# The output projection of a gated mix of FNet and sliding-window attention, by Strassen's scheme on pairs of blocks instead of block by block

## The chip, the cores and the metric

The kernel runs on one core of one Trainium2 chip. The metric is device time in microseconds of that core, median of three runs. Engines are named as in the profile: PE is TensorE, PEld its weight loads, DVE VectorE, ACT ScalarE, POOL GpSimd, SP SyncE (which issues DMAs). L528 is line 528 of the kernel before; of the changed kernel, lines are a little higher where the same code moved (L528 is L529 there, L453 is L454, L587 is L588).

## The reference

With S = 2048 positions of D = 512, 32 heads of 16 and a causal window of 256:

```python
a = x @ dft_hid_re.T;  b = x @ dft_hid_im.T
y = dft_seq_re @ a - dft_seq_im @ b            # FNet
q, k, v = heads(x @ wqkv)
p = softmax(where(0 <= i - j < 256, q k^T / 4, -1e9))
attn = (p @ v) @ wo                            # sliding-window attention
g = sigmoid(sum(x * gate_w))
out = g * y + (1 - g) * attn
```

## The kernel before, in words

All data are fp32, kept as two parts: `hi`, the value cast to the matmul's fp32r type, and `lo`, the rest (`lo = x - hi`). A product takes three matmuls, `hi hi`, `hi lo`, `lo hi`: TERMS. A "split" is a cast (L80 on ACT, L82 on DVE) and a subtraction on DVE (L85).

PE's order is written out by hand (a manual schedule of PE alone; the other engines' orders come from the scheduler, and each engine runs its own in turn). It weaves two streams. The **dense** stream has the projections of x, then `y`: for each block of 128 positions 16 chunks of three matmuls of 512 columns (`c_part`, L528, result `dc`). The pieces of the DFT matrices `cr` and `ci` (512 KB each) are loaded to `raw`, a pair of buffers, and split there to `hi` and `lo` by jobs between matmuls (L115 and L116, in the profile at L587 `late`). The **attention** stream walks over 128 blocks `n` (4 groups of 8 heads by 16 blocks of the sequence, two heads at a time): `s_pair` (L366) for block n, and for block k = n - LAG, `t_pair` (L448), whose probabilities `pt` or `home` are written by ACT (L449) and masked by POOL's affine selects (L453, L457). Every six blocks a visit of `pv` (L474) multiplies them with `vpad`, into which POOL spreads v (L431). `make_pad` (L349, DVE) writes the pads that `s_pair` and `t_pair` read. The attention's output goes to DRAM (`o_scr`), and the sum of gate times `y` to `r_scr` or, where the projection is ahead, to `mixed`.

The loop of attention ends with `attention_done`: `wo` (512 by 512, as two halves of 512 KB) is loaded through `raw`, split on DVE into `fin`, which takes the place of `ring0`, a buffer of attention's own; `os` takes that of `ring1`. From then on `FIN` is set, and `c_part` calls `tail_step()` ahead of every four chunks, that is every 12 dense matmuls. A tail step runs `wo_block` for up to two blocks: 12 matmuls of 128x512 each (4 head groups by TERMS, L811) into a bank of PSUM of `ps_a`, then on DVE `r = (1 - g) * ps + r` (L813), and the block's 256 KB go out by SP. Then it prepares more blocks (`wo_prep`: the block of `o_scr` is loaded, ACT casts it, DVE subtracts). Blocks 15 and 14 go first of those still missing their `y`, so that their attention part stands ready. The last block of `y` ends in two column halves of 256 (`c_final`, L558, 12 matmuls), whose two results are added at L560 and leave on SP's and ACT's queues (L561).

Of the kernel before, what the change touches and what calls it, by code (L numbers as in the profile page):

```python
# [7 lines left out]
F32 = mybir.dt.float32  # L8
F32R = mybir.dt.float32r
AF = mybir.ActivationFunctionType  # L10
OP = mybir.AluOpType
# [21 lines left out]
def fnet_window_mix(ctx: ExitStack, tc: tile.TileContext, xT, x, wqk, wv, wr, wi, cr, ci, wo, gw, out):  # L33
# [509 lines left out]
    def c_final(get, ab):  # L543
        ps = ps_d.tile([P, 512], F32, name="dc", tag="d")
        g = g1[:, 15:16]
        for j in range(2):
            w = get((1, 30 + j))
            yield from c_part(w, range(16)[8 * j:8 * j + 8 - 2 * j], ab, ps, (0, 13))
            yield
        while wait:  # L550
            tail_step()
        r = mixed.pop(15)
        late(nc.vector.scalar_tensor_tensor, r, ps, g, r, OP.mult, OP.add)
        for c, dma in ((slice(0, 256), nc.sync), (slice(256, 512), nc.scalar)):
            ps2 = ps_a.tile([P, 512], F32, name="t", tag="st")
            for i in (14, 15):
                for a, b in TERMS:
                    nc.tensor.matmul(ps2[:, c], w[a][:, i % 8 * 128:i % 8 * 128 + 128], ab[SC[i]][:, b, c],  # L558
                                     start=i == 14 and a + b == 0, stop=i == 15 and a == 1)
            nc.vector.scalar_tensor_tensor(r[:, c], ps2[:, c], g, r[:, c], op0=OP.mult, op1=OP.add)  # L560
            dma.dma_start(out[15][:, c], r[:, c])  # L561
        yield
# [22 lines left out]
    def late(fn, *args):  # L585
        with behind("act", "dve"):
            return fn(*args)  # L587
# [172 lines left out]
    now = []  # L760
    wait = []
    mixed = {}
    born = {}
    clock = iter(range(99))

    def tail_step():
        t = next(clock)
        for tb in [tb for tb in O if born[tb] < t - 2][:2]:
            if tb in wait:
                wait.remove(tb)  # L770
                ld(out[tb], wo_block(tb, 1))
            else:
                mixed[tb] = wo_block(tb, 0)
        for tb in (*wait[:5], 15, 14, *wait[5:]):
            if tb not in O and tb not in mixed and len(O) < 7 and (tb > now[-1] or tb in wait):
                wo_prep(tb)
                born[tb] = t

    def attention_done():
        fin = const.tile([P, 8192], F32R, name="fin", tag="ring0")  # L780
        ORAW.extend(f(fin[:, 4112 + 512 * i:4624 + 512 * i]).rearrange("p (g t) -> p g t", g=NG) for i in range(7))
        fin = fin[:, 16:4112].rearrange("p (j c h e) -> p j c h e", j=2, c=2, h=2)
        OS.append(const.tile([P, 8, 2, NG, P], F32R, name="os", tag="ring1"))
        for j in range(2):
            raw = st.tile([P, 1024], F32, name="raw", bufs=2)
            ld(raw, wo[j])
            for c in range(2):
                split(fin[:, j, c, 0], fin[:, j, c, 1], raw[:, c * 512:c * 512 + 512])
        FIN.append(fin)

    OS = []
    ORAW = []
    O = {}
    slot = iter(range(99))

    def wo_prep(tb):
        oraw = ORAW[0]
        ORAW.append(ORAW.pop(0))
        ld(oraw, o_scr[tb // 4][:, :, tb % 4 * P:tb % 4 * P + P].rearrange("g p t -> p g t"))
        O[tb] = OS[0][:, next(slot) % 8]  # L800
        split(O[tb][:, 0], O[tb][:, 1], oraw[:], True)

    def wo_block(tb, half):
        o = O.pop(tb)
        r = ev.tile([P, 512], F32, name="ev")
        ld(r, r_scr[half if half or tb < 16 - SWITCH else 2][tb])
        ps = ps_a.tile([P, 512], F32, name="t", tag="st")
        n = 0
        for g in range(NG):
            for a, b in TERMS:  # L810
                nc.tensor.matmul(ps, o[:, a, g], FIN[0][:, g // 2, g % 2, b], start=n == 0, stop=n == 11)  # L811
                n += 1
        nc.vector.scalar_tensor_tensor(r, ps, g0[:, tb:tb + 1], r, op0=OP.mult, op1=OP.add)  # L813
        return r


    stream = dense()
# [39 lines left out]
    def v_next(n):  # L857
        if n < N:
            for c in range(2):
                need(("v", n % NB // 2 + c))  # L860
            with behind(*(("sp",) if n < 8 else ())):
                v_load(n)

    for n in range(N + LAG + 1):
        k = n - LAG
        if k == 0:
# [8 lines left out]
        for p in range(NP):  # L875
# [11 lines left out]
            if visit:  # L887
                for j in range(summed, k):
                    pv(j)
                summed = k  # L890
                if k < N:
                    t_pair(k, p)
            for at_n, at_p, do in TURN if n > 12 else FIRST:
# [61 lines left out]
```

## Time and profile before

| | us |
|---|---|
| median of 3 runs (lowest to highest) | 851.23 (850.59 to 851.45) |
| the profiled execution, own time | 850.96 |
| its span in the trace | 849.0 |
| PE busy | 843.7 (99%) |
| DVE, ACT, POOL busy | 611.3, 593.6, 256.8 |
| output projection, first and last matmul of L811 | 774.0 to 837.2, x192 |

The page's first part gives each engine's busy time. PE's matmuls overlap in the pipeline, so the duration of one (392 ns for 512 columns) is not the time that it takes from the stream; that is the distance between two starts. The granted clock is that of TensorE, 1.00 at full speed. A row of the chain of waits says from when on, and for how long, an instruction group was what the end waited for. A row of the timeline has start, length, engine, line, operation, tiles, shapes and count.

### The profile page before, as it was taken

What the parts mean: (1) busy time and instruction counts of PE and PEld (TensorE: products, weight loads), DVE (VectorE), ACT (ScalarE), POOL (GpSimd) and SP (SyncE); (2) the same over time, 40 slices, a digit from 0 to 9 for tenths busy, and PEclk for the clock granted to TensorE, in tenths of its full rate; (3) what the DMA queues carried; (4) which work ended last, traced back from release to release, by engine and by line L of the source; (5) the groups of instructions that cost most, each with busy time, mean ns of one, the idle gap of its engine ahead of it and who ended that gap; (6) DMA issues with size and microseconds to landing.
All of it is one profiled execution on the core that took longest, in us unless ns stands there. A gap on an engine that the chain in (4) does not pass through costs nothing.

```text
span 849.0 us, 16711 instructions
## 1 busy us (share of the span) xinstructions
PE 843.7 (99%) x5166; PEld 691.4 (81%) x5166; DVE 611.3 (72%) x1999; ACT 593.6 (70%) x1798; POOL 256.8 (30%) x578
## 2 busy tenths in 40 slices
PE   9999999999999999999999999999999999999998
PEld 6888888888888788888888887888887878878887
DVE  5588978667978787787787886887987864437531
ACT  6488888878888897787877886877777865532100
POOL 8102332233332233342323333343233364620000
PEclk9999999999999999999999999999999999999999
DMA  8776678476765275533454557969774435339732
GB/s 296 244 228 186 214 243 257 181 233 225 216 222 178 63 211 134 171 115 123 137 158 127 177 150 227 308 216 306 254 215 134 138 121 164 128 118 333 225 134 75
DMA packets 94345, 160.99 MB, mean 190 GB/s; under 512 B 26800, under 2 KB 35760, under 8 KB 94256
## 3 DMA queue, kind: packets, MB, share of 16 engines
q1 hardware_dynamic: 93824, 159.28, 60.2%
q8 instruction: 40, 0.66, 0.3%
q10 hardware_dynamic: 432, 0.66, 0.2%
q14 instruction: 49, 0.40, 0.1%
HBM read 108.27 MB, written 51.64 MB: 188 GB/s over the span
## 4 chain that ended last, share of the span: by engine, by line
PE 94%; DMA 2%; DVE 2%; issue 1%; SPq 0%; ACT 0%; DVEq 0%; ACTq 0%
PE dc L528 39%; PE dqk L280 9%; PE dab L303 9%; PE t L448 9%; PE s L366 8%; PE o L474 8%; PE t L811 5%; PE dv L303 5%; DMA raw<-wo 1%; DMA ev<-l_scr 1%; PE s L268 1%; DVE sm L368 1%; PE dv L592 0%; SPq L56 0%; DVE pad L349 0%
## 5 line engine op out<-in xcount | busy, mean ns | idle before, releaser
L528 PE MATMUL dc<-big,hi 128*128 128x512 f32 x1020 | 344.5, 393 | 0.0
L371 ACT ACTIVATE sm<-sm,ml 128x320 f32<-128x320 f32 (+4 forms) x512 | 277.4, 543 | 59.6 <-DVE ml L368 54.1
L368 DVE CUSTOM_DVE_ANT_0 sm<-s,mask 128x320 f32<-128x320 f32 (+4 forms) x512 | 235.0, 464 | 108.6 <-PE s L366 73.2
L449 ACT ACTIVATE pt<-t 128x320 f32<-128x320 f32 (+4 forms) x392 | 159.8, 411 | 87.7 <-PE t L448 82.1
L528 PE MATMUL dc<-big,lo 128*128 128x512 f32 x510 | 200.3, 393 | 0.0
L528 PEld LDWEIGHTS dc<-big,hi 128*128 128x128 f32 x1020 | 180.4, 188 | 22.6
L448 PE MATMUL t<-ring,pad 128*128 128x320 f32 (+4 forms) x512 | 156.8, 306 | 0.1
L453 POOL TENSOR_SCALAR_AFFINE_SELECT pt<-pt 128x128 f32<-128x128 f32 x196 | 71.2, 363 | 283.3 <-ACT pt L449 279.7
L366 PE MATMUL s<-ring,pad 128*128 128x320 f32 (+4 forms) x512 | 155.3, 303 | 0.3 <-DVE ml L368 0.2
L349 DVE TENSOR_SCALAR pad<-ring,half 96x256 fp32r<-96x256 f32 x384 | 120.4, 360 | 11.9 <-PE t L448 11.7
L448 PEld LDWEIGHTS t<-ring,pad 128*128 128x128 f32 x512 | 96.1, 188 | 31.1 <-issue 8.7
L366 PEld LDWEIGHTS s<-ring,pad 128*128 128x128 f32 x512 | 96.2, 188 | 21.7 <-DVE ml L368 2.0
L528 PEld LDWEIGHTS dc<-big,lo 128*128 128x128 f32 x510 | 95.9, 188 | 11.9
L371 ACT ACTIVATION_READ_ACCUMULATOR sm<-sm,ml 128x1 f32 x512 | 97.4, 190 | 0.0
L587 DVE TENSOR_TENSOR lo<-raw,hi 128x512 fp32r<-128x512 f32 x137 | 93.8, 694 | 0.1
L303 PE MATMUL dab<-hi,big 128*128 128x512 f32 x256 | 89.0, 394 | 0.0
L280 PE MATMUL dqk<-big,hi 128*128 128x512 f32 x240 | 85.0, 393 | 0.0
L431 POOL TENSOR_SCALAR vpad<-vr,half 128x256 f32<-128x256 f32 x64 | 61.3, 969 | 65.3 <-PE o L474 30.3
L587 DVE CAST hi<-raw 128x512 fp32r<-128x512 f32 x137 | 57.7, 431 | 20.5 <-PE dc L528 17.0
L347 ACT ACTIVATE pad<-ring,half 96x256 fp32r<-96x256 f32 x128 | 66.8, 522 | 0.0
L457 POOL TENSOR_SCALAR_AFFINE_SELECT pt<-pt 128x128 f32<-128x128 f32 x172 | 60.8, 354 | 0.0
L474 PE MATMUL o<-pt,vpad 128*32 128x320 f32 (+4 forms) x1072 | 57.7, 351 | 0.0
(96 smaller groups left out, 912.5 us busy)
## 6 DMA issues: line engine op xcount, KB each, us to landing
qk_scr<-home SPq DMA_DIRECT2D x32, 512.0 KB
ring<-qk_scr SPq DMA_DIRECT2D x32, 512.0 KB
raw<-cr SPq DMA_DIRECT2D x32, 512.0 KB
raw<-ci SPq DMA_DIRECT2D x32, 512.0 KB
r_scr<-ev SPq DMA_DIRECT2D x42, 256.0 KB
ev<-r_scr SPq DMA_DIRECT2D x42, 256.0 KB
ab_scr<-home SPq DMA_DIRECT2D x20, 512.0 KB
big<-ab_scr SPq DMA_DIRECT2D x20, 512.0 KB
```

Of the source, the lines that this page charges most:

```text
L280: nc.tensor.matmul(ps, w[a][:, c:c + 128], XT[dk, ss][:, b], start=n == 0, stop=n == 11)
L303: nc.tensor.matmul(ps, XT[dk, ss][:, a, c * 128:(c + 1) * 128], wh[b], start=n == 0, stop=n == 11)
L349: nc.vector.tensor_scalar(dst, src, half[:96, h:h + 1], None, op0=OP.mult)
L366: nc.tensor.matmul(ps[:, :w], PAD[0, n][:, p], ring[1][:, p, k0:k0 + w], start=True, stop=True)
L368: mark("dve", nc.vector.tensor_tensor_reduce(out=sm[:, :w], in0=ps[:, :w], in1=mask[:, WIN - w:], scale=1.0, scalar=3e38, op0=OP.add, op1= ...
L371: mark("act", nc.scalar.activation(sm[:, :w], sm[:, :w], AF.Exp, bias=nm[:, c], scale=-1.0, accum_out=l[:, c]))
L448: nc.tensor.matmul(ps[:, :w], PAD[1, n][:, p], ring[0][:, p, q0:q0 + w], start=True, stop=True)
L449: nc.scalar.activation(pt[:, p, :w], ps[:, :w], AF.Exp, scale=-1.0)
L453: nc.gpsimd.affine_select(a, a, pattern=[[0, 2], [2, 64]], compare_op=OP.is_ge, fill=0.0, base=1, channel_multiplier=-1)
L474: nc.tensor.matmul(OT[g, sb][32 * p:32 * p + 32, q - sb * 512:e - sb * 512], v2[:, p], pt[:, p, q - q0:e - q0], start=first, stop=kb == 8 ...
L528: nc.tensor.matmul(ps, w[a][:, i % 8 * 128:i % 8 * 128 + 128], ab[SC[i]][:, b], start=i == ends[0] and a + b == 0, stop=i == ends[1] and a ...
L587: return fn(*args)
```

## The change

The output projection is done for pairs of blocks (0 and 1 the first two finished, 15 and 14 the third pair, eight in all). The attention output of a pair, 256 by 512, times `wo`, 512 by 512, is seen as a 2x2 by 2x2 product of halves (128 positions by 256 by 256) and done in Winograd's form of Strassen's scheme: 7 products instead of 8. A product is 2 (chunks of 128 in the inner dimension) times 3 (TERMS) matmuls of 128x256, so a pair takes 42 of them instead of 24 of 128x512. Four sums of the operand's halves, s1 to s4, are made on POOL (`sums`) and the seven operands split (ACT's casts, DVE's subtractions) into columns of ring0 and ring1; the seven weight operands are made once: four differences for each of the two chunks of the inner dimension on POOL (`wo_diffs`, L827), and in all 14 casts and 14 subtractions on DVE (`fin_split`). The products are combined on the way to the result: ACT copies p1 to `u` (L934), DVE adds p6 to it (L936), and `into` (L928) adds with the gate to `r`, seven times a pair.

A pair is begun in one tail step (`wo_begin`, 24 matmuls, products p1, p6, p7, p5 in four banks) and ended in the next one (`rest`, 18 matmuls that go on in three of these banks); the steps are listed in `BEGIN`. The sums are issued three steps earlier, the splits one step, the loads of the attention output four.

What `attention_done` did is moved ahead: `wo` is fetched chunk by chunk (2 x 256 KB each) in blocks 114 and 117 of k (through `raw`, in turn with the pieces of `ci`), its differences and splits follow in blocks 115 to 120 into columns of the rings that attention has left, the first pair is loaded, summed and split in blocks 121 to 123 (`BEFORE_END`). From `FIN` on the casts of the dense stream's pieces are done by ACT instead of DVE. The result of a pair is kept in `rt` (in place of `home`), the operand in buffers that `vpad` and the pads leave.

```diff
-            jobs.append(lambda c=c: late((nc.vector if masks else nc.gpsimd).tensor_copy, hi[:, c], raw[:, c]))
+            jobs.append(lambda c=c: late(nc.scalar.copy if FIN else (nc.vector if masks else nc.gpsimd).tensor_copy,
+                                         hi[:, c], raw[:, c]))
...
     def tail_step():
         t = next(clock)
-        for tb in [tb for tb in O if born[tb] < t - 2][:2]:
-            if tb in wait:
-                wait.remove(tb)
-                ld(out[tb], wo_block(tb, 1))
-            else:
-                mixed[tb] = wo_block(tb, 0)
-        for tb in (*wait[:5], 15, 14, *wait[5:]):
-            if tb not in O and tb not in mixed and len(O) < 7 and (tb > now[-1] or tb in wait):
-                wo_prep(tb)
-                born[tb] = t
+        for i in range(8):
+            if t == BEGIN[i] + 1:
+                wo_end(i)
+        for i in range(8):
+            if i and t == max(0, BEGIN[i] - 3):
+                wo_sums(i)
+            if i and t == BEGIN[i] - 1:
+                wo_split(i)
+            if t == BEGIN[i]:
+                wo_begin(i)
+            if i > 3 and t == BEGIN[i] - 4:
+                wo_load(i)
+
+    BEGIN = 1, 3, 4, 6, 7, 9, 10, 12
...
+    def wo_fetch(c):
+        RAW[c] = st.tile([P, 1024], F32, name="raw", bufs=2)
+        for j in range(2):
+            ld(RAW[c][:, HALVES[j]], wo[j][:, HALVES[c]])
+
+    def wo_diffs(c):
+        b11, b12, b21, b22 = quarters(RAW[c], 4)
+        tw = [const.tile([P, 512], F32, name="tw", tag=f"pad0_{b}") for b in range(2)]
+        t1, t3, t2, t4 = (q for t in tw for q in quarters(t, 2))
+        for t, x, y in ((t1, b12, b11), (t3, b22, b12), (t2, b22, t1), (t4, b21, t2)):
+            nc.gpsimd.tensor_sub(t, x, y)
+        DIFF[c] = b11, b21, b22, t4, t1, t2, t3
...
+    def sums(s1, s2, s3, s4, a, b):
+        nc.gpsimd.tensor_add(s1, b[:, :256], b[:, 256:])
+        nc.gpsimd.tensor_sub(s3, a[:, :256], b[:, :256])
+        nc.gpsimd.tensor_sub(s2, s1, a[:, :256])
+        nc.gpsimd.tensor_sub(s4, a[:, 256:], s2)
...
+    def wo_split(i):
+        if i > 1:
+            r_load(i)
+        split_a(i)
+        s = EX[i][:, :1024].rearrange("p (m t) -> p m t", m=4)
+        n = 3 if i % 2 else 4
+        split(*halves(spots(1, n, COL[i % 2])), s[:, :n], True)
+        if i % 2:
+            split(*halves(os_spot(6, 1)), s[:, 3], True)
...
+        def product(ps, m, n, start=True):
+            o = os_spot(m, i % 2).rearrange("p (h c t) -> p h c t", h=2, c=2)
+            for c in range(2):
+                for a, b in TERMS:
+                    nc.tensor.matmul(ps, o[:, a, c], fin(n, b, c), start=start and c == 0 and a + b == 0,
+                                     stop=c == 1 and a == 1, skip_group_check=True)
+
+        def into(r, t, g):
+            nc.vector.scalar_tensor_tensor(r, t, g, r, op0=OP.mult, op1=OP.add)
...
+        product(p1, 0, 0)
+        nc.scalar.copy(u, p1)
+        product(p6, 4, 5)
+        nc.vector.tensor_add(u2, p6, u)
+        product(p7, 5, 6)
+        into(r2[:, hi], p7, gb)
+        product(p5, 3, 4)
+        into(r2[:, hi], p5, gb)
+        into(r1[:, hi], u2, ga)
+        into(r2.rearrange("p (n e) -> p n e", n=2), u2.unsqueeze(1).to_broadcast([P, 2, 256]), gb)
+
+        def rest():
+            product(p1, 1, 1, False)
+            into(r1[:, lo], p1, ga)
+            product(p7, 2, 3, False)
+            into(r2[:, lo], p7, gb)
+            product(p5, 6, 2, False)
+            into(r1[:, hi], p5, ga)
...
+    BEFORE_END = {(121, 1): first_load, (122, 0): first_sums, (123, 0): lambda: split_a(0), (123, 2): first_split}
+    for c, k in enumerate((115, 118)):
+        BEFORE_END |= {(k - 1, 1): lambda c=c: wo_fetch(c), (k, 1): lambda c=c: wo_diffs(c),
+                       (k + 1, 0): lambda c=c: fin_split(c, (0, 1)), (k + 1, 2): lambda c=c: fin_split(c, (2, 4)),
+                       (k + 2, 0): lambda c=c: fin_split(c, (6, 5, 3))}
```

Three places in the engines' orders, where a row is line, operation, result and operands, shape, and how many alike follow each other.

PE in the tail, before: one tail step's 24 matmuls of the projection (two blocks), between the last and the next dense matmuls.

```order
L528 MATMUL dc<-big,lo 128x512
L811 MATMUL t<-fin,os 128x512 x24
L528 MATMUL dc<-big,hi 128x512 x2
L528 MATMUL dc<-big,lo 128x512
```

After, at the first pair: its 24 in one step and its 18 in the next, with 12 dense ones between (`ring_267` and `ring_268` are ring0 and ring1, which hold both operands).

```order
L529 MATMUL dc<-big,lo 128x512
L924 MATMUL t<-ring_267 128x256 x6
L924 MATMUL t<-ring_268 128x256 x18
L529 MATMUL dc<-big,hi 128x512 x2
...
L529 MATMUL dc<-big,lo 128x512
L924 MATMUL t<-ring_267 128x256 x12
L924 MATMUL t<-ring_267,ring_268 128x256 x6
```

The projection's first matmuls stand two tail steps earlier than before, in pieces of 24 and 18 narrower ones.

POOL in attention's blocks 112 to 115, before: the selects of `home` and of `pt`, then the spread of v.

```order
L457 AFFINE_SELECT home<-home 128x2x64
L453 AFFINE_SELECT pt<-pt 128x2x64
L457 AFFINE_SELECT pt<-pt 128x2x64
L453 AFFINE_SELECT pt<-pt 128x2x64
L457 AFFINE_SELECT pt<-pt 128x2x64
L431 TENSOR_SCALAR vpad_303<-vr,half 128x16x16 x2
```

After: the four differences of the first chunk of `wo` (`tw`, from `raw`) stand among them.

```order
L458 AFFINE_SELECT home<-home 128x2x64
L827 TENSOR_TENSOR tw<-raw 128x256
L454 AFFINE_SELECT pt<-pt 128x2x64
L458 AFFINE_SELECT pt<-pt 128x2x64
L827 TENSOR_TENSOR tw<-raw 128x256
L827 TENSOR_TENSOR tw<-raw,tw 128x256
L454 AFFINE_SELECT pt<-pt 128x2x64
L458 AFFINE_SELECT pt<-pt 128x2x64
L827 TENSOR_TENSOR tw<-raw,tw 128x256
L432 TENSOR_SCALAR vpad_303<-vr,half 128x16x16 x2
```

One difference is now ahead of the first of these selects of `pt`, three are ahead of the second, four ahead of the spread.

PE where pair 1 ends and pair 2 (blocks 15 and 14) begins in the same tail step, after:

```order
L529 MATMUL dc<-big,lo 128x512
L924 MATMUL t<-ring_267 128x256 x24
L924 MATMUL t<-ring_268 128x256 x18
L529 MATMUL dc<-big,hi 128x512 x2
```

And DVE around the same kind of place, where pair 3 ends and pair 4 begins: the results are emptied from PSUM (L928 with `t`) between the subtractions for the dense piece (`lo`) and for the operands (`ring`).

```order
L928 SCALAR_TENSOR_TENSOR rt<-pt,g_306,rt 128x512
L85 TENSOR_TENSOR ring_268<-pt,ring_268 128x3x256
L588 TENSOR_TENSOR lo<-raw,hi 128x512
L928 SCALAR_TENSOR_TENSOR rt<-t,g_306,rt 128x256
L588 TENSOR_TENSOR lo<-raw,hi 128x512
L928 SCALAR_TENSOR_TENSOR rt<-t,g_306,rt 128x256
L85 TENSOR_TENSOR ring_267<-oraw,ring_267 128x2x256
L85 TENSOR_TENSOR ring_267<-oraw,ring_267 128x256
L928 SCALAR_TENSOR_TENSOR rt<-t,g_306,rt 128x256
L85 TENSOR_TENSOR ring_267<-pt,ring_267 128x256
L936 TENSOR_TENSOR pt<-t,pt 128x256
```

Nothing but an L813 (result), the operand's L85 and the piece's L587 stood there before; the three L928 with `t` are now what frees the banks for the pair that follows.

More of the change, by code (lines that the diff above doesn't have):

```diff
@@ L549, in c_final @@
             yield
-        while wait:
+        while O:
             tail_step()
@@ new lines, in halves, with quarters @@
+    def halves(t):
+        return (t[:, :256], t[:, 256:]) if len(t.shape) == 2 else (t[:, :, :256], t[:, :, 256:])
+    RAW = {}
+    DIFF = {}
+    def quarters(t, m):
+        return [t[:, k * 256:k * 256 + 256] for k in range(m)]
+    def wo_fetch(c):
[9 more added lines that the diff above has]
+        DIFF[c] = b11, b21, b22, t4, t1, t2, t3
@@ new lines, in fin_split @@
+    def fin_split(c, ms):
+        for m in ms:
+            split(fin(m, 0, c), fin(m, 1, c), DIFF[c][m])
+    def attention_done():
+        RT.append(const.tile([P, 6, 512], F32, name="rt", tag="home"))
+        new = []
+        for tag in ("vpad0", "vpad1", "pad1_0", "pad1_1"):
+            t = const.tile([P, NG, P], F32, name="oraw", tag=tag)
+            new.append(t[:].rearrange("p g t -> p (g t)"))
+        ORAW[:0] = new
+        r_load(0)
+        wo_load(1)
+        r_load(1)
+        for i in range(2, 4):
+            wo_load(i)
+        FIN.append(True)
@@ L792, in fnet_window_mix @@
+    RT = []
     ORAW = []
     O = {}
[L794 to L814, printed above, removed]
+    R = {}
@@ L817, in fnet_window_mix, with wo_end @@
+    def wo_end(i):
+        O.pop(i)()
     stream = dense()
```

86 lines of the change are left out of this document (74 added, 12 removed).

## The prediction

> **What bounds the kernel now.** I read the page's sums first, then its chain of work.
>
> ```profile
> span 849.0 us, 16711 instructions
> PE 843.7 (99%) x5166; PEld 691.4 (81%) x5166; DVE 611.3 (72%) x1999; ACT 593.6 (70%) x1798; POOL 256.8 (30%) x578
> PE 94%; DMA 2%; DVE 2%; issue 1%; SPq 0%; ACT 0%; DVEq 0%; ACTq 0%
> ```
>
> PE is busy 843.7 of 849.0 us and holds 94% of the chain, so a gain has to be PE time that is no longer issued. The change touches two stages, so next come the windows of 10 us (PE, PEld, DVE, ACT, POOL busy, then clock, DMA share, GB/s).
>
> ```profile
> 700.00:710.00 10.00, 10.00 (x113) 7.52 (x112) 3.48 (x8) 4.22 (x10) 4.53 (x11) 1.00 0.65 216
> 710.00:720.00 10.00, 10.00 (x50) 8.62 (x49) 5.83 (x12) 6.50 (x15) 5.07 (x13) 1.00 0.36 99
> 720.00:730.00 10.00, 10.00 (x64) 7.85 (x66) 3.81 (x8) 5.61 (x13) 4.21 (x12) 1.00 0.49 172
> 770.00:780.00 10.00, 9.88 (x44) 7.83 (x43) 7.81 (x15) 2.46 (x5) 0.00 (x0) 1.00 1.09 328
> 780.00:790.00 10.00, 10.00 (x46) 8.21 (x45) 8.39 (x14) 2.82 (x6) 0.00 (x0) 1.00 1.11 358
> 800.00:810.00 10.00, 10.00 (x45) 8.26 (x44) 4.66 (x8) 1.24 (x2) 0.00 (x0) 1.00 0.31 105
> 830.00:840.00 10.00, 10.00 (x46) 8.23 (x45) 1.67 (x3) 0.00 (x0) 0.00 (x0) 1.00 0.30 115
> 840.00:849.00 9.00, 5.82 (x32) 4.88 (x30) 1.72 (x3) 0.00 (x0) 0.00 (x0) 0.97 0.09 29
> ```
>
> In attention's last blocks and in the tail alike PE is full, and the granted clock is 1.00. POOL does nothing in the tail, ACT little, DVE falls from 8.39 to 1.67. So the tail has room beside PE for more elementwise work, and no room on PE: what PE is spared there shortens the end, what it is made to wait lengthens it.
>
> **The PE term.** Next the chain in the tail (start, length, what), and the first two groups of the output projection in the timeline.
>
> ```profile
> 780.08 2.74 PE dc L528 x12
> 782.82 5.50 PE t L811 x24
> ...
> 832.10 5.50 PE t L811 x24
> ```
>
> ```profile
> 774.01 6.06 PE L811 MATMUL t<-fin,os 128*128 128x512 f32 x24
> 782.65 5.66 PE L811 MATMUL t<-fin,os 128*128 128x512 f32 x24
> ```
>
> ```profile
> L811 PE MATMUL t<-fin,os x192: 388/392/503, 774.0 to 837.2; 128*128 128x512 f32 x192
>   DVE fin L85: 0.5, 1
> ```
>
> 24 matmuls of 512 columns take 5.50 us on the chain, 0.229 each (the 392 ns are latency, they overlap). The 192 of them are 192 × 0.229 = 44.0 us. The new 256-wide matmul has one twin: the last 12 of before's program, which also bring a fresh 128x128 weight each.
>
> ```profile
> 844.23 0.40 PE L558 MATMUL t<-big,hi 128*128 128x256 f32 x2
> 844.46 0.28 PE L558 MATMUL t<-big,lo 128*128 128x256 f32 x1
> 844.46 0.31 PEld L558 LDWEIGHTS t<-big,hi 128*128 128x128 f32 x2
> ...
> 845.54 0.28 PE L558 MATMUL t<-big,lo 128*128 128x256 f32 x1
> ```
>
> The first starts at 844.23, the twelfth at 845.54: 1.31 / 11 = 0.119, and from the third on the steps are 0.120. 8 pairs × 42 = 336, × 0.120 = 40.3 us. So Strassen's eighth fewer products is worth not 12.5% of 44.0 but 44.0 − 40.3 = **3.7 us**, since a 256-wide matmul costs 0.524 of a 512-wide one.
>
> **The start of the tail.** The first group of before is 0.40 us longer than the second (6.06 against 5.66): it waited for the last split of `wo`, the 0.5 us of "DVE fin L85". In the changed kernel the weights and pair 0 are ready by then: **−0.4**. Next in line there are the raw Ci pieces, as before, and the banks of PSUM, which are all free at the first pair.
>
> **Attention's end.** Here the change adds, between blocks 115 and 123: on DVE 14 casts and 14 subtractions of 128x256 for `wo`, on POOL 8 subtractions for `wo` and 4 sums of the first pair, on SP the loads of `wo` among the raw pieces. The nearest rows:
>
> ```profile
> L163 DVE TENSOR_TENSOR lo<-pt,hi 128x256 fp32r<-128x256 f32 x4 | 2.1, 526 | 0.0
> L82 DVE CAST fin<-raw 128x512 fp32r<-128x512 f32 x4 | 1.5, 423 | 3.8 <-DMA raw<-wo 3.8
> L587 POOL TENSOR_TENSOR lo<-raw,hi 128x512 fp32r<-128x512 f32 x5 | 6.6, 1332 | 0.0
> ```
>
> DVE: a subtraction between half of the 512-wide one and 0.526, a cast between 0.21 and 0.42; the sum is 14 × (0.56 to 0.95) = 8 to 13 us, and the idle time of 710 to 730 is 4.17 + 6.19 = 10.4. It fits, but it moves what stands behind it: the pads of blocks 116 and 118, which PE's `t` matmuls wait for. POOL: a 256-wide subtraction is an estimate of 0.67 (half of 1.33). The wait of PE most at risk exists in before already, small; the waits of 690 to 760, then POOL's and PE's rows:
>
> ```profile
> PEld o L474 <- POOL pt L453: 0.7, 2, 0.4
> ```
>
> ```profile
> 704.73 0.39 POOL L453 TENSOR_SCALAR_AFFINE_SELECT pt<-pt 128x128 f32<-128x128 f32 x1 [1.05 <-ACT pt L449]
> 705.07 0.74 POOL L457 TENSOR_SCALAR_AFFINE_SELECT pt<-pt 128x128 f32<-128x128 f32 x1
> 707.82 1.82 POOL L431 TENSOR_SCALAR vpad<-vr,half 128x256 f32<-128x256 f32 x2 [2.02 <-issue]
> ```
>
> ```profile
> 707.98 0.72 PE L474 MATMUL o<-pt,vpad 128*32 128x320 f32 x8
> ```
>
> Selects of block 113 end at 705.81, and the last 8 matmuls of that visit of `pv` use them from 707.98: 2.2 us of slack. POOL's new order, shown with the change, puts three subtractions ahead of the last selects, 3 × 0.67 = 2.0, and the first of them waits for the chunk of `wo` that must land first. Lost there: nothing to 2 us. At the pads of 116 and 118 another nothing to 1 us. I take **+0.5** for both, near the lower end, as the slack covers POOL's work at the estimated duration.
>
> The GPSIMD Engine Reference of the Trainium skill, section "Specifications", says that POOL shares its SBUF interfaces with VectorE and meets contention with DVE instructions of two SBUF inputs. The selects here agree: 0.39 and 0.74 with the same shape, the long one beside DVE's subtractions at 704.27. By that rule the three subtractions would take up to 1.3 each, and the +0.5 becomes about +2.
>
> **The tail's elementwise work.** A pair costs DVE the `lo` of 1792 columns, one 256-wide addition, six 256-wide and one 512-wide `into`.
>
> ```profile
> L813 DVE SCALAR_TENSOR_TENSOR ev<-t,g,ev 128x512 f32<-128x512 f32 x16 | 12.0, 748 | 26.4 <-PE t L811 26.4
> L85 DVE TENSOR_TENSOR os<-fin,os 128x512 fp32r<-128x512 f32 x16 | 10.5, 682 | 1.1 <-ACT os L80 1.1
> L560 DVE SCALAR_TENSOR_TENSOR ev<-t,g,ev 128x256 f32<-128x256 f32 x2 | 1.0, 484 | 0.2
> ```
>
> 1792 / 512 × 0.682 = 2.4; 0.53; 6 × 0.484 = 2.9; 0.75: 6.6 us. Two pairs run in three tail steps: PE's time there is 3 × 2.74 of dense (twelve matmuls each) and 2 × 42 × 0.120 = 10.1, together 18.2 us. DVE has 13.2 for the pairs and some 2.5 for the dense stream (1.5 pieces' two subtractions, three quarters of a 0.75 addition; the piece's casts go to ACT): 15.7 of 18.2. ACT and POOL have more room: per pair ACT casts 1792 columns and copies 256, POOL does four sums, under 3 us each. So this is hidden: 0. Tightest are the three places where a pair's 18 last matmuls are followed at once by the next pair's 24 (the last rows shown with the change): the next pair takes the banks that DVE has just to empty, with under 1 us to spare.
>
> **The end.**
>
> ```profile
> 845.28 1.06 DVE L560 SCALAR_TENSOR_TENSOR ev<-t,g,ev 128x256 f32<-128x256 f32 x2
> 845.79 0.33 SPq L561 DMA_DIRECT2D out<-ev  x1
> 846.37 0.35 ACTq L561 DMA_DIRECT2D out<-ev  x1
> ```
>
> Before, the last full block left at 838.4, well ahead of the two halves at 845.79 and 846.37. Now blocks 12 and 13, 256 KB each, are issued about 1 us ahead of them, since the last pair ends just before the 12 final matmuls. At the 328 to 358 GB/s of the busy windows 0.5 MB needs 1.5 us: +0 to +1.5; I take **+0.5**, as part is through by then.
>
> **Sum.** −3.7 − 0.4 + 0.5 + 0.5 = −3.1. The profiled execution took 850.96 (span 849.0 and 2.0 around it), 0.27 under the median of 851.23: 850.96 − 3.1 = 847.9, and from the median 848.1. I say **848.0**. Own range, with the bounds above: 846.9 (no loss) to 849.5.
>
> **Rivals.**
> - *Selects and pads come late at attention's end.* PE waits 2 to 4 us there instead of 0.5; time 849.5 to 851.5. For it: POOL's strict place ahead of the selects, DVE's 10.4 us of idle time against 8 to 13. Against: before's own waits there are 0.4 at most.
> - *DVE becomes the tail's bound at the bank handovers (slower side).* It decides from 18.2 us of DVE work in three steps, that is 1.25 more per pair than my 6.6. If a 256-wide operation costs what a 512-wide one does (0.75 and 0.68), a pair costs 6 × 0.27 + 3 × 0.15 = 2.1 more, three steps 19.9, and PE loses 1.7 × 4 = 6.8 over eight pairs: 848.0 + 6.8 = 855, or 852 with half of it. Against it: L560 with 0.484.
> - *The weight load binds at 256 columns.* If the next load could not overlap the running matmul, each step would be the load's 0.19 (0.31 for two that overlap) plus about 0.02: 336 × 0.21 = 71 us, and 878. Twelve steps of 0.120 speak against it, with no sign of drift. TensorE: Matmul & The Clock Gate of the Trainium skill, Part 3, "The mechanism", says that a weight load overlaps matmuls in flight only when their row groups differ; all rows here are full. The L558 rows disagree with that reading; its queue would have to have hidden twelve loads.
>
> **Chances.** About 0.2% (1.7 us) is what a measurement of this kernel can tell from no change. Forecast 0.64 (faster). Late selects and pads 0.20: mostly within 0.2%, 0.18 and 0.02 slower. DVE in the tail 0.12, weight load 0.02, and 0.02 for the end's transfers with both stalls: slower. Faster 0.64, same 0.18, slower 0.18. The range leaves out the last three cases and holds the first two: 846.9 to 851.7.
>
> **What would show it.** 336 matmuls at L924 with starts 0.120 apart; no PE idle time but the end's in the windows after 770; the waits naming no "PEld o" after POOL over 0.5 us between 705 and 735, and none of PE for L928. I am wrong if L924's groups of 24 take over 2.9 us, if L827 takes over 1 us, or if L928 holds PE where pairs 2, 4 and 6 (counted from 0) begin.

## The result, and the profile after

The changed kernel takes 854.98 us (median, 853.73 to 856.77) against 851.19 (849.81 to 851.76): 1.005 times as long, 95% interval 1.0036 to 1.0064. It is slower by some 3.8 us, where I forecast 3.1 less. The profiled execution took 853.73.

The page first: PE's busy time fell and its share of the chain too, while DVE's and DMA's shares of the chain have grown and POOL has come into it.

```profile
span 851.6 us, 17176 instructions
PE 842.0 (99%) x5310; PEld 697.2 (82%) x5310; DVE 646.4 (76%) x2071; ACT 609.6 (72%) x1832; POOL 296.9 (35%) x618
PE 88%; DVE 5%; DMA 3%; issue 1%; POOL 1%; SPq 1%; ACT 0%; DVEq 0%; ACTq 0%; POOLq 0%
```

Windows of 10 us again (PE, PEld, DVE, ACT, POOL busy, then clock, DMA share, GB/s). In the kernel before, PE was full, 10.00, in each of these stretches.

```profile
700.00:710.00 10.00, 9.52 (x107) 6.63 (x106) 7.33 (x16) 3.58 (x9) 6.86 (x11) 1.00 0.41 138
710.00:720.00 10.00, 9.83 (x48) 8.16 (x47) 7.88 (x19) 6.17 (x15) 7.42 (x12) 1.00 0.51 170
720.00:730.00 10.00, 7.33 (x35) 5.99 (x35) 9.96 (x22) 3.27 (x8) 7.53 (x13) 1.00 0.50 172
780.00:790.00 10.00, 9.88 (x61) 8.70 (x59) 6.60 (x12) 3.70 (x7) 8.02 (x9) 1.00 0.38 123
790.00:800.00 10.00, 9.44 (x62) 8.43 (x63) 9.10 (x17) 3.19 (x8) 5.07 (x6) 1.00 0.46 158
800.00:810.00 10.00, 10.00 (x64) 9.02 (x63) 8.86 (x15) 3.71 (x8) 4.96 (x6) 1.00 0.58 185
```

Two places: attention's last blocks, where DVE is busy 9.96 of the worst 10 us, and the tail around 790. Next what PE waited for, between 690 and 770 (total, times, longest), and in the tail.

```profile
PE t L449 <- DVE pad L350: 2.7, 1, 2.7
PEld o L475 <- POOL pt L458: 1.1, 1, 1.1
PEld o L475 <- POOL pt L454: 0.7, 2, 0.4
```

```profile
PEld t L924 <- DVE rt L928: 1.6, 4, 0.6
PE t L924 <- DVE rt L928: 0.7, 3, 0.4
```

(PEld's longest wait there, 3.1 with `issue` as its end, is the same stall as the 2.7 of `t`.) To put sizes on both places, I set matmul against matmul of the two traces. The first 690 us differ by −1.0 us (in the runs below it is between −1.2 and +1.4, though all that they change comes later). From there to attention's last `t` matmul the changed kernel falls back by **5.3 us**: 1.2 in the visit of `pv` ahead of block 114, 0.3 at block 116, 2.8 at block 118, 0.7 in the next visit, ahead of block 120, and 0.2 between. In the tail, groups of L924 take **2.0 us** more than their count times 0.120. These two losses are the measure of every experiment below. The first has some scatter: e4, e5 and e9 keep the orders of DVE, ACT and POOL at attention's end as in the change, and lost 6.0, 5.7 and 6.5 there.

How the 2.8 come about, on DVE (the rows between are of the same kinds):

```profile
717.68 0.29 DVE L82 CAST ring<-raw 128x256 fp32r<-128x256 f32 x1 [2.06 <-DMA raw<-wo]
718.01 0.85 DVE L85 TENSOR_TENSOR ring<-raw,ring 128x256 fp32r<-128x256 f32 x1
...
721.88 1.39 DVE L588 CAST hi<-raw 128x512 fp32r<-128x512 f32 x2
...
724.48 0.37 DVE L350 TENSOR_SCALAR pad<-ring,half 96x256 fp32r<-96x256 f32 x1
```

```profile
725.00 0.38 PE L449 MATMUL t<-ring,pad 128*128 128x320 f32 x1 [2.67 <-DVE pad L350]
```

The pad that `t` of block 118 needs stands in DVE's queue behind most of the split of wo's second chunk. DVE first waits for that chunk, then works without a pause until 724.48. And how the 1.2 come about, on POOL and PE:

```profile
703.68 1.21 POOL L827 TENSOR_TENSOR tw<-raw 128x256 f32<-128x256 f32 x1 [2.66 <-DVE hi L588]
...
707.77 0.34 POOL L458 TENSOR_SCALAR_AFFINE_SELECT pt<-pt 128x128 f32<-128x128 f32 x1
```

```profile
708.16 0.73 PE L475 MATMUL o<-pt,vpad 128*32 128x320 f32 x4 [0.48 <-POOL pt L458]
```

In the tail, PE where the second pair ends (18) and the third begins (24), with what each idle time waited for:

```profile
789.01 0.87 PE L924 MATMUL t<-ring 128*128 128x256 f32 x6
790.03 2.47 PE L924 MATMUL t<-ring 128*128 128x256 f32 x18 [0.15 <-DVE rt L928]
792.87 0.98 PE L924 MATMUL t<-ring 128*128 128x256 f32 x6 [0.37 <-DVE rt L928]
794.01 1.85 PE L924 MATMUL t<-ring 128*128 128x256 f32 x12 [0.15 <-DVE rt L928]
```

From 789.01 to the next dense matmul at 795.70 it is 6.69 us instead of 5.03: 1.65 of the 2.0. Another 0.4 is at the handover to the fifth pair, none at the last.

### The profile page after: what moved, and what is told of

Read it like the earlier page. It is cut to its first block, busy times and chain, and to the rows that moved or that the text cites. A ratio compares the mean times of both kernels' runs of the same rounds, so it can differ in the third digit from the quotient of the medians.

```text
span 851.6 us, 17176 instructions
## 1 busy us (share of the span) xinstructions
PE 842.0 (99%) x5310; PEld 697.2 (82%) x5310; DVE 646.4 (76%) x2071; ACT 609.6 (72%) x1832; POOL 296.9 (35%) x618
## 4 chain that ended last, share of the span: by engine, by line
PE 88%; DVE 5%; DMA 3%; issue 1%; POOL 1%; SPq 1%; ACT 0%; DVEq 0%; ACTq 0%; POOLq 0%
PE dc L529 36%; PE dab L304 9%; PE dqk L281 9%; PE s L367 8%; PE t L449 8%; PE o L475 7%; PE dv L304 5%; PE t L924 3%; DMA oraw<-o_scr 1%; DVE ring L85 1%; PE s L269 1%; DVE lo L588 1%; DMA raw<-ci 1%; DVE ring L82 1%; SPq L56 1%
## 5 line engine op out<-in xcount | busy, mean ns | idle before, releaser
L588 DVE CAST hi<-raw 128x512 fp32r<-128x512 f32 x126 | 54.5, 439 | 11.7 <-PE dc L529 8.4
```

## The experiments

The theories after the result. **P**: at attention's end each loss is one strict queue in which the preparation stands ahead of attention's own work and waits for a late input. Its parts at first: **A1**, POOL's subtractions slow DVE and hold back the selects; **A2**, wo's second chunk lands late. Rival: the engines have too little time there. In the tail, **C1**: the third pair's inputs come late, its split stands in DVE's queue ahead of the emptying of banks; later narrowed to **S**: it is POOL's sums. Rival **C2**: the handover of banks is too tight for DVE in any case.

All in one table; losses are read from each run's trace, ratios are to the kernel before, run beside it. e1, e2 and e13 leave parts of the work out, as said there.

| run | us | ratio, 95% | attention's end | tail |
|---|---|---|---|---|
| the change | 854.98 | 1.005 (1.0036 to 1.0064) | 5.3 | 2.0 |
| e1_no_wo_prep | 850.18 | 0.9991 (0.9980 to 1.0002) | 0.0 | 1.7 |
| e2_no_diffs | 850.87 | 1.0006 (0.9995 to 1.0017) | 1.5 | 2.0 |
| e3_own_place | 856.01 | 1.0065 (1.0044 to 1.0086) | 7.5 | 2.4 |
| e4_swap | 859.38 | 1.0107 (1.0074 to 1.0139) | 6.0 | 5.6 |
| e5_even_steps | 857.38 | 1.0088 (1.0073 to 1.0103) | 5.7 | 3.6 |
| e6_pads_first | 855.97 | 1.0072 (1.0057 to 1.0087) | 5.2 | 2.2 |
| e7_pads_selects_first | 856.27 | 1.0071 (1.0055 to 1.0088) | 7.8 | 2.8 |
| e8_all | 859.50 | 1.0112 (1.0097 to 1.0128) | 7.8 | 3.9 |
| e9_later_pairs | 856.69 | 1.0068 (1.0042 to 1.0093) | 6.5 | 2.2 |
| e10_three_queues | 849.85 | 0.9987 (0.9974 to 0.9999) | 0.0 | 2.2 |
| e11_three_queues_later | 849.71 | 0.9987 (0.9973 to 1.0000) | 0.4 | 2.0 |
| e12_order | 850.76 | 1.0000 (0.9984 to 1.0016) | 0.0 | 2.4 |
| e13_no_sums | 847.65 | 0.9965 (0.9953 to 0.9977) | 0.4 | 0.1 |
| e14_sums_in_order | 848.99 | 0.9983 (0.9974 to 0.9992) | 0.4 | 0.7 |
| e15_order_old_steps | 848.13 | 0.9976 (0.9964 to 0.9989) | 0.6 | 0.5 |
| e16_spread | 847.52 | 0.9971 (0.9959 to 0.9983) | 0.2 | 0.0 |

Part of the larger losses is PE's clock and not a wait. In e3 to e8, once each, the granted clock was 0.50 instead of 1.00 for 3.4 us (6.8 in e7 and e8) around a stall of PE, and dense matmuls then started 0.43 us apart instead of 0.23. At attention's end this makes some 1.6 us of the loss of e3 and of e5, 1.7 of e6's, 2.9 of e7's and 2.1 of e8's. In e4 it falls into the tail, where the dense matmuls and the step from them to a group lost another 1.3 us, which the column of the tail, L924's groups alone, does not hold. In the change and all other runs the clock was 1.00 through attention's end and the tail up to the last matmul, also after the change's longest stall. What decides it no run here shows: it fell around 1.86 us of idle PE in e6, and did not after 2.67 in the change.

### Attention's end

```diff
 e1: -    for c, k in enumerate((115, 118)):
     -        BEFORE_END |= {(k - 1, 1): lambda c=c: wo_fetch(c), ...
 e2: -            nc.gpsimd.tensor_sub(t, x, y)
     -        DIFF[c] = b11, b21, b22, t4, t1, t2, t3
     +        DIFF[c] = b11, b21, b22, b12, b11, b12, b21
 e3: +        if c: RAW[c] = [const.tile([P, 512], F32, name="wr", tag=f"pad0_{b}") for b in range(2)]
     -        BEFORE_END |= {(k - 1, 1): lambda c=c: wo_fetch(c),
     +        BEFORE_END |= {(114 - 2 * c, 1): lambda c=c: wo_fetch(c),
```

> Leaves out the preparation of wo (its loads, the 8 differences on POOL, 14 casts and 14 subtractions on DVE); the projection multiplies by what the rings last held. The first pair's preparation stays. Read from the two traces, attention's end lost 5.3 us and the tail's PE 2.0 us at two handovers of banks. Theory A (the loss at attention's end is wo's preparation): that loss falls to 0.7 or less (the first pair's share), the tail is unchanged, so about 850.4 (851.2 - 3.7 - 0.4 + 2.0 + 0.7 + some tenths). Rival B (it is the first pair's sums, or the other queues' new order): the loss stays at 4 or more, 853.5 to 855.

The loss is 0.0, so wo's preparation is its cause. The first pair's work is all there and holds up nothing; that its share in the change came from being pushed back behind wo's is how I read it, no run shows it alone. The tail's loss stays (1.2 and 0.4 at the same two handovers), so the two are separate.

> Leaves out the 8 subtractions of wo on POOL (the raw quarters are split in place of the differences); DVE's 28 operations and wo's loads stay. Theory A1 (POOL's subtractions hold back the selects and, sharing their way to memory, slow DVE beside them by about 2.3 us ahead of the pad of block 118): the stalls of pv at block 113 (1.2) and of t at block 118 (2.8) both shrink to under 0.5, the loss at attention's end to about 1.5, the time to about 851. Theory A2 (the second chunk of wo lands too late and DVE waits for it ahead of that pad): pv's stall goes, the 2.8 stays at 2 or more, the time is about 853.

1.5, as A1 has it in sum, not in its parts: pv's stalls are gone, but 1.4 of the 2.8 at block 118 stay. DVE still waits for the chunk (2.50 us, to 716.99) and puts that pad at 722.09 instead of 724.48. So POOL's eight subtractions, by their place in its queue and by what they cost DVE together, account for 3.8 of 5.3, about half of the 2.8 among them, and a piece is left to A2 or to DVE's order.

> The second chunk of wo gets its own place (two pads that are free by then) instead of a raw buffer, and is loaded two blocks ahead of the first chunk; the differences go to the buffers of sm and to mask. All computation stays, at the same blocks. Theory A2 (late landing): DVE no longer waits for this chunk, the stall of t at block 118 falls from 2.8 to under 0.5, loss 5.3 to about 2.3, time about 852. Theory A1 (POOL beside DVE): DVE's operations stay slow, the stall falls by half at most, time 853 to 854.5.

A2 falls as I had put it. DVE does not wait for the chunk any more, block 118 does not stall, but block 116 does, by 4.1 at once and 5.7 with the lower clock behind it. The scheduler, which sees the chunk ready earlier, has put its whole split ahead of the pad of block 116:

```profile
715.05 0.94 DVE L85 TENSOR_TENSOR ring<-sm,ring 128x256 fp32r<-128x256 f32 x2
715.91 1.39 DVE L588 CAST hi<-raw 128x512 fp32r<-128x512 f32 x2
717.23 0.74 DVE L743 SCALAR_TENSOR_TENSOR ev<-dc,g,ev 128x512 f32<-128x512 f32 x1
717.88 1.37 DVE L588 TENSOR_TENSOR lo<-raw,hi 128x512 fp32r<-128x512 f32 x2
719.18 0.28 DVE L82 CAST ring<-mask 128x256 fp32r<-128x256 f32 x1
719.38 0.34 DVE L350 TENSOR_SCALAR pad<-ring,half 96x256 fp32r<-96x256 f32 x1
```

With no wait in these rows the pad comes some 4 us after it was needed: what counts is its place in the queue. Hence the next runs, which fix that place (the last of them also brings the first pair two blocks later).

```diff
 e6: +  last["pad"] = <the pad's DVE instruction>
     +  with behind("pad"): split(fin(m, 0, c), fin(m, 1, c), DIFF[c][m])
 e7: e6 and  last["sel"] = <the second select>;  with behind("sel"): <wo's differences, the first pair's sums>
 e10: e7 and last["exp"] = <the exponential>;  with behind("pad", "exp"): <the first pair's splits>
     -  (121, 1): first_load, (122, 0): first_sums, (123, 0): ... split_a(0), (123, 2): first_split
     +  (121, 1): first_load, (123, 0): first_sums, (124, 0): ... split_a(0), (125, 2): first_split
```

> The casts and subtractions of wo on DVE are ordered behind the latest pad (written in the program before them) instead of where the scheduler put them; POOL and all else as in the change. Theory P (what costs at blocks 116 and 118 is the place of the pads in DVE's queue, behind wo's work, whatever makes that work slow): the stalls of t there (0.3 and 2.8, and the 4 us that the run with the chunk's own place lost at 116) fall under 0.3 together; pv's 1.2 and 0.7 stay; loss 2.0 of 5.3, time about 851.7. Rival (DVE simply has too much to do between 705 and 732): the delay comes back as a wait for the dense pieces or for later pads, loss 4 or more, 854.

Blocks 116 and 118 lose nothing now, and DVE had the time. Of pv's stalls the 1.1 stays, the 0.7 does not show; a new one comes at block 121, 2.0 of waiting and 1.7 at the lower clock (waits from 725 to 745):

```profile
ACT ring L80 <- DMA oraw<-o_scr: 7.5, 1, 7.5
...
PE t L449 <- ACT pt L450: 1.9, 1, 1.9
```

ACT stands at the cast of the first pair, whose attention output now arrives later (its place is the one that wo's differences leave), and the exponentials of block 121 stand behind that cast. It is the same mechanism in a third queue. I had looked at two. Without the lower clock e6 loses 3.5, so the order on DVE did gain, though the time does not show it.

> As the run before, and POOL's differences of wo and the first pair's sums are ordered behind the latest selects. Theory P for both queues: pv's stalls go as well, attention's end loses 0.5 or less, the tail 2.0 as before: about 850 (851.2 - 3.7 - 0.4 + 2.0 + 0.5 and some tenths). Rival (what is pushed back holds the raw buffers longer, and the dense pieces of ci come late): a new wait for raw of 1.5 us or more, 852.

pv's stalls are gone too, and the wait in ACT's queue has grown (4.9 at once at block 121; the rest of the 7.8 is the lower clock) as the first pair comes later still.

> wo's work and the first pair's are ordered behind attention's on all three queues: DVE's behind the latest pad, POOL's behind the latest selects, ACT's casts of the first pair behind the latest exponentials, and the first pair's sums and splits come two blocks later. The runs that did so on DVE and POOL alone lost 5.2 and 7.8 at block 121, where ACT's exponentials stood behind the first pair's casts. Theory P (each loss is one strict queue in which the preparation stands ahead of attention's own work and waits for a late input): attention's end loses 0.5 or less, the tail 2 to 2.5; about 850.3. Rival (the engines lack the time): a new wait of 2 us or more appears there, 853 or more.

The loss is 0.0 with all of the work in place. PE is full through attention's end again, with DVE at 8.19 and POOL at 10.00 of 10 us (the columns as above):

```profile
710.00:720.00 10.00, 10.00 (x50) 8.60 (x49) 7.82 (x18) 6.83 (x16) 8.46 (x13) 1.00 0.33 108
720.00:730.00 10.00, 10.00 (x55) 8.20 (x57) 6.22 (x15) 6.06 (x14) 10.00 (x20) 1.00 0.36 114
730.00:740.00 10.00, 10.00 (x113) 7.96 (x103) 8.19 (x24) 4.61 (x11) 6.12 (x6) 1.00 0.94 299
```

P is shown for the three queues together, "too little time" is refuted: the engines could always do this work there, only not ahead of attention's. For the first pair two things changed at once, the order on ACT and the two blocks that it comes later; which of them cures block 121 is not separated. (The 5.2 in the expectation is all that e6 lost; at block 121 it was 3.7.)

### The tail

```diff
 e4: -  pair = [15, 14] if i == 2 else ...     +  pair = [15, 14] if i == 3 else ...
 e5: -  if FIN and i % 4 == 0:  BEGIN = 1, 3, 4, 6, 7, 9, 10, 12      (each end one step after its begin)
     +  if FIN and i % 2 == 0:  BEGIN = 2, 5, 8, 11, 14, 17, 20, 23   (each end two steps after)
 e9: +  BEGIN = 1, 4, 5, 7, 8, 10, 11, 12
 e13: e11 without the sums of pairs 1 to 7;   e14: e11 and
     +  with behind("sum"): <s1 to s4>;  last["sum"] = <s4>
```

> Blocks 15 and 14 become the fourth pair instead of the third; nothing else. Their attention output is the last to reach DRAM, so the third pair's sums came late and its splits fell into the handover to it (1.65 us lost there, 0.4 at the next). Theory C1 (late inputs): with early blocks as the third pair the first handover loses under 0.5, both together 0.8 or less, attention's end unchanged, about 853.7. Rival C2 (a handover is too tight by itself, DVE cannot empty the banks in time): 2.0 as before or more, time unchanged at 855.

The handover to the third pair loses 0.0 instead of 1.65, as C1 says, so a handover as such is not too tight, though PE comes to it some 6 us later for the stall ahead of it. But the second pair's data, behind more loads now, come later (its sums start at 775.02 after a wait of 8.7 for the load, 771.19 and 5.8 in the change). Its split and the dense piece's then stand ahead of the emptying of the first pair's banks: 4.9 us, part of it at the lower clock:

```profile
784.27 0.97 PE L924 MATMUL t<-ring 128*128 128x256 f32 x6 [3.42 <-DVE rt L928]
```

> Tail steps come every 6 dense matmuls instead of 12; each pair begins 3 such steps after the one before and ends 2 after its begin, so 6 dense matmuls (1.36 us) stand between a pair's end and the next one's begin. Same work, attention's end untouched (5.3 lost). Rival C2 (a handover without dense work between is too tight for DVE): the tail's loss of 2.0 falls to 0.3 or less, about 853.3. Theory C1 (the third pair's inputs come late and its splits stand in DVE's queue ahead of the emptying): 1 us or more of it stays at the first or second handover, 854 or more.

3.6: the waits have moved to the first three pairs (0.6 at the first one's end, 1.8 and 1.3 in the begins of the second and third), although dense work stands between them. Of these only the second begins earlier than in the change, by 6 dense matmuls. C2, as the price of a handover without dense work, is out.

> Only the list of steps: BEGIN is 1, 4, 5, 7, 8, 10, 11, 12, so that pairs 1 to 6 begin one tail step (about 4.9 us) later, with one handover more, at the last pair. Attention's end untouched (5.3 lost). Theory C1 (the second and third pair's inputs come late; the even steps, which began them earlier, lost 3.6 instead of 2.0): the tail's loss falls from 2.0 to 0.6 or less, about 853.5. Rival C2 (handovers cost by themselves): four handovers lose 2.0 or more, 855 or more.

Of the four handovers only the first, to the third pair, loses: still 2.25, though it comes a step later. "Late inputs" alone does not tell why. The next profile does (the kernel with three queues ordered and these steps, e11, POOL's sums and then DVE):

```profile
774.50 1.45 POOL L878 TENSOR_TENSOR pt<-oraw 128x256 f32<-128x256 f32 x1
775.92 0.73 POOL L879 TENSOR_TENSOR pt<-oraw 128x256 f32<-128x256 f32 x1
776.62 1.19 POOL L881 TENSOR_TENSOR pt<-oraw,pt 128x256 f32<-128x256 f32 x1
777.77 1.62 POOL L880 TENSOR_TENSOR pt<-pt,oraw 128x256 f32<-128x256 f32 x2
779.34 0.92 POOL L878 TENSOR_TENSOR pt<-oraw 128x256 f32<-128x256 f32 x1
780.23 1.43 POOL L881 TENSOR_TENSOR pt<-oraw,pt 128x256 f32<-128x256 f32 x2
```

```profile
782.08 1.37 DVE L85 TENSOR_TENSOR ring<-pt,ring 128x1024 fp32r<-128x1024 f32 x1 [2.02 <-ACT ring L80]
783.37 2.37 DVE L588 TENSOR_TENSOR lo<-raw,hi 128x512 fp32r<-128x512 f32 x2
```

POOL works on the sums of the second to the fifth pair by turns (L878 to L881 are s1, s3, s2, s4), so the third pair's s4 is done only at about 781 (ACT's cast of it starts at 781.00). DVE idles 2 us for it, then has 14 us of work without a gap, in which the emptying of PSUM stands late.

> On the kernel with the three queues ordered and the later steps: the four sums of pairs 1 to 7 on POOL are left out (raw quarters are split in their place, as many casts and subtractions). Theory S (the tail's remaining 2.0, all at the handover from the second to the third pair, comes from POOL's sums: 12 operations of 1.0 to 1.7 us in a mixed order, behind which DVE's split of the third pair waits, and beside which DVE's own operations double): that loss falls under 0.4, about 848. Rival C2 (DVE has too much work there, with or without POOL): 1.2 us or more stays, 849 or more.

0.1: it is POOL's sums. This run also splits the quarters one by one (128x256, where the others split up to 128x1024 at once) and has its operands earlier, so it does not tell the sums' order from their mere work; the next run does. (Their durations in e11 are 0.73 to 1.72 us, not 1.0 to 1.7.)

> On the same kernel: each pair's sums on POOL are ordered behind the whole of the pair before, instead of those of pairs 2 to 4 mixed. All computation stays. Theory S (order): the third pair's last sum is done about 4 us earlier (781.2 before), the loss at that handover falls from 2.1 to 0.6 or less, about 848.3. If it is POOL working beside DVE as such (contention) and not its order: 1.5 or more stays.

The third pair's s4 (L882 here) and its split on DVE:

```profile
777.37 0.81 POOL L882 TENSOR_TENSOR pt<-oraw,pt 128x256 f32<-128x256 f32 x1
...
779.93 1.36 DVE L85 TENSOR_TENSOR ring<-pt,ring 128x1024 fp32r<-128x1024 f32 x1
```

In pair order s4 ends at 778.18 (about 781 in e11), the split at 781.29 (783.45). As this trace is 1.5 us later than e11's at attention's end, both are some 4 us earlier, and the loss falls from 2.0 to 0.7. Order is most of it. What the remaining 0.7 is stays open. It goes without the sums (e13), but also with all of them when the third pair begins one tail step earlier (e15 below). In e14 the dense piece's two subtractions on DVE (from 790.12 on) stand between the emptyings of that handover, in e15 they come behind them.

### Both

```diff
 e8:  e7, e5's steps, the first pair's splits behind "pad", the second pair's oraw in the pads' buffers
 e11: e10 and BEGIN = 1, 4, 5, 7, 8, 10, 11, 12
 e12: e11 and
     -  for tag in ("vpad0", "vpad1", "pad1_0", "pad1_1"):
     +  for tag in ("pad1_0", "pad1_1", "vpad0", "vpad1"):
 e15: the change, e10 and e14's order of sums
 e16: e15 and, as in e5, steps of 6 dense matmuls, BEGIN = 2, 8, 11, 13, 16, 18, 21, 23
```

> Both orders at attention's end, the even steps in the tail, the first pair's splits behind the pads as well, and the second pair's operands in the pads' buffers (free earlier than those of vpad). If both causes are as the theories have it: attention's end loses 0.5 or less, the tail 0.5 or less: 851.2 - 3.7 - 0.4 + 1.0 = about 848. If the tail's late inputs still bind: 849 to 850.

Run before ACT's queue was understood: block 121 cost 5.6 at once in it, 7.8 with the lower clock, and the tail's even steps 3.9.

> The three queues ordered and the later list of steps together. If both theories (P and C1) hold: attention's end loses 0.5 or less, the tail 0.6 or less: 851.2 - 3.7 - 0.4 + 1.1 + some tenths = about 848.5. If the queues still lack time: 852 or more.

Attention's end as expected, the tail not (2.0): C1 had left out POOL's order.

> The run before, and the second pair's attention output goes to the pads' buffers, which attention leaves earlier than those of vpad (the trace shows its second load issued only at 766.56). If the second pair's inputs are still late in the run before, this gains up to what they cost there; if not, the same time within 0.3.

2.4 in the tail: no gain, so the second pair's inputs cost nothing that shows.

> The change with all four orders (three queues at attention's end, sums in order in the tail) and its own list of steps. Theory S: the first handover, one tail step earlier than in the run before, loses 0.3 to 1.3 (1.2 in the run with three queues alone), the second 0.4; about 849. If late inputs no longer count at all: 848.3.

The handover to the third pair loses 0.0, where I expected 0.3 to 1.3; the one to the fifth loses 0.4 as expected, and 0.2 is at the first pair's end. e10 differs from this run in the order of the sums alone and lost 1.2, 0.4 and 0.65 at these places, 2.2 in all instead of 0.5. This is S once more, with the change's own steps.

> All four orders, and steps of 6 dense matmuls with the pairs begun at 2, 8, 11, 13, 16, 18, 21, 23: the second pair as late as in the later list, 1.36 us of dense work between its end and the third pair's begin. If order alone cures the tail: the same as the sums in order, 848.3, within 0.4. If DVE still needs time at that handover: 0.5 to 1.4 less than there.

With all four orders the change's own steps lose 0.5 in the tail, the spread ones nothing: PE waits for nothing there any more, though three of its pairs still follow the one before at once, and its windows of 10 us from 770 to 840 stand at 10.00. 847.52 us is 3.0 less than the kernel before beside it (850.54), 0.9971 (0.9959 to 0.9983), and the shortest time of the kernels that leave nothing out; from e15 its interval does not separate it.

The chain of its page, and the window that holds the worst handover of the others:

```profile
PE 97%; DVE 1%; DMA 1%; issue 0%; ACT 0%; SPq 0%; DVEq 0%; ACTq 0%
```

```profile
780.00:790.00 10.00, 10.00 (x67) 9.13 (x66) 9.40 (x15) 3.27 (x7) 9.76 (x10) 1.00 0.44 143
```

## Why the prediction was wrong

- **PE's term held.** 336 matmuls, a group of 24 in 2.87 us, of 42 in 5.03 where nothing held it, so 0.120 each and −3.7 by the groups. The weight-load rival is out: if a load overlapped a running matmul only where the row groups differ, as "The mechanism" in Part 3 of TensorE: Matmul & The Clock Gate of the Trainium skill has it in one sentence, it would have been 878. The rows disagree with that sentence through the whole tail; the section's other case, a load into the background weight buffer, they do not contradict.
- **The start of the tail held** (−0.4: the first group takes 2.87 like the others).
- **Attention's end failed: "I take +0.5 for both, near the lower end, as the slack covers POOL's work at the estimated duration".** It was 5.3, beyond the rival's 2 to 4 as well, though that rival, late selects and pads, had the mechanism: 1.9 are at the selects, 3.2 at the pads of blocks 116 and 118. Two things were wrong in that step. The durations: POOL's differences took 0.77 to 1.21 instead of 0.67, and DVE's own operations beside them up to twice as long; POOL's side I had named in a sentence (+2) and kept the lower end, DVE's side I had not. And, more, the form of the argument: I set DVE's added 8 to 13 us against 10.4 us of idle time and wrote "It fits". It did fit (e10 loses nothing with it). What cost was which instruction stood behind it, in a strict queue with late inputs. I named the pads behind it, but priced them at nothing to 1 us, with slacks worked out from durations without contention. ACT's queue, which I did not look at, cost little in the change and most in e6 and e7.
- **The tail's "So this is hidden: 0" failed by 2.0.** DVE's sum was about right (6.6 us a pair, some 6.8 by the same rows after; 9.10 of 10 us busy at worst), and the handovers, named as tight, were not the cause by themselves. POOL's sums were: priced by their amount (under 3 us a pair; 3.9 in the mean after), not by when the third pair's would be ready in the order that POOL runs them.
- **The end held better than the sum had it:** from the last matmul's start to the span's end it is 3.5 us before (849.0 − 845.54) and after (851.6 − 848.05), at most +0.1 for my +0.5.
- The sum by measured terms is −3.7 − 0.4 + 5.3 + 2.0 + 0.1 = +3.3, against +3.6 in the trace from 690 us on (2.6 and the 1.0 gained ahead of it) and +3.8 between the medians. The 0.3 between the first two is in the dense matmuls: from attention's last `t` on, the 200 matmuls outside the projection take 41.27 us instead of 40.95; why is not shown.
- The first rival came true and more; of the second came the wait for L928, not its cause, too much work for DVE. I had given the two 0.32 and only 0.14 of that to "slower", as each was priced alone. Of my signs of being wrong at least two came: L827 took over 1 us, and L928 held PE where pairs 2 and 4 begin, not pair 6.
- Three slips in the working, none of which decides: the bounds of the terms (2 and 1 at attention's end, 1.5 at the end, over 846.9) add to 851.4, not 849.5; PE's three tail steps are 18.3 us; and both selects of the contention sentence, the short one too, lie beside DVE's subtractions at 704.27, so they do not show what I took from them.

## What to carry to other kernels

Work moved under a full engine isn't free because the helpers have idle time: ask, for each helper's queue, which instruction of the critical stream now stands behind it, and when the input of the moved one arrives. Order the moved work behind the stream's own on every queue that it touches: here the order on DVE alone, and on DVE and POOL, left a wait in ACT's queue. Order it in itself, too, by when each result is needed, as POOL's sums show. And price two engines' elementwise work in one stretch at the contended duration.

## What the runs showed of the hardware beyond that

In these rows POOL and DVE both work on SBUF operands, and one of the two takes about twice as long, now this one, now that. The changed kernel, first DVE, then POOL:

```profile
706.70 0.96 DVE L85 TENSOR_TENSOR ring<-raw,ring 128x256 fp32r<-128x256 f32 x1
709.05 0.41 DVE L85 TENSOR_TENSOR ring<-raw,ring 128x256 fp32r<-128x256 f32 x1
```

```profile
706.59 0.79 POOL L827 TENSOR_TENSOR tw<-raw,tw 128x256 f32<-128x256 f32 x1
708.97 3.44 POOL L432 TENSOR_SCALAR vpad<-vr,half 128x256 f32<-128x256 f32 x2
```

The same subtraction of DVE takes 0.96 beside a subtraction of POOL and 0.41 beside POOL's spread of v, but then the spread takes 3.44 us for two, where it took 1.82 before (at 707.82). A cast of 128x256 on DVE takes 0.83 at 704.20, beside a subtraction of POOL, and 0.28 at 709.39, beside the spread. Section "Specifications" of the GPSIMD Engine Reference of the Trainium skill names this contention for DVE operations with two SBUF inputs or in a 2-port perf mode. The rows of the subtractions, which have two SBUF inputs, agree; the casts have one, and whether they ran in such a mode no row here shows.
